# An earlier activation table and earlier masks, a smaller source of zeros, and eight identity products ahead of the loop, in a gated recurrence with a top-k expert layer

## The chip, the cores and the metric

The kernel runs on one core of a Trainium2 chip. A core has five engines with a queue of their own each: TensorE (PE in the profile, with its weight loads as PEld), VectorE (DVE), ScalarE (ACT), GpSimd (POOL) and SyncE (SP). Here SyncE computes nothing; its queue issues almost all DMA transfers. The metric is the device time of one execution in microseconds (us), as the median of several runs; lower is better.

## The reference: what is computed

The first stage is a gated linear recurrence over 4 sequences of 5056 steps and 256 channels; the second treats its 4 x 5056 = 20224 results as tokens of a layer with 8 experts, where each expert keeps only the 80 tokens with the highest gate.

```python
def _attn_ref(x, f_logit, lower_bound):
    sig = 1.0 / (1.0 + np.exp(-f_logit))
    f = lower_bound[None, None, :] + (1.0 - lower_bound[None, None, :]) * sig
    i = 1.0 - f
    for t in range(S):
        h = f[:, t] * h + i[:, t] * x[:, t]
        y[:, t] = h

def _moe_ref(x, w_gate, w1, w2, capacity):          # x: (20224, 256), capacity 80
    logits = x @ w_gate                              # 8 experts
    expert_idx = np.argmax(logits, axis=1)
    gate_w = softmax(logits)[np.arange(N), expert_idx]
    out = np.zeros((N, D))
    for e in range(E):
        tok_idx = np.where(expert_idx == e)[0]
        tok_idx = tok_idx[np.argpartition(-gate_w[tok_idx], capacity)[:capacity]]
        h = np.maximum(x[tok_idx] @ w1[e], 0.0)      # w1[e]: 256 x 1024
        out[tok_idx] = gate_w[tok_idx, None] * (h @ w2[e])   # w2[e]: 1024 x 256
```

All values are 32-bit floats. At most 640 of the 20224 rows of the output are not zero, so the kernel writes zeros over the whole output, 20.7 MB, and then scatters the experts' rows over them.

## The kernel before

**Recurrence.** The work is cut into 40 units: 10 groups of up to 512 steps, times 4 sequences. A unit is a pair of loads, `f_t` and `x_t`, 512 KB each (448 KB in the last group), `load` at lines 214 to 221. Then `gate` (ScalarE: sigmoid, line 225), `enter` (GpSimd: product with x, line 229), `to_channels` (TensorE: 8 transposes of each through the identity into PSUM tiles `sp` and `up`, line 236), `decay` (ScalarE, line 247), `scan` (VectorE: the recurrence itself, line 253, into `h_all`, which stays on the chip) and `logits` (TensorE, line 265). The loop at lines 404 to 422 writes the order out by hand: in turn n it loads unit n + 3, gates n + 2, transposes n + 1, scans n. The pool of loads has four buffers for each of the two tiles, so a fifth load waits until the transposes have read the first.

**Before the loop.** `setup` at lines 186 to 212 prepares constants: VectorE scales the gate weights by `omlb`, which waits for two small loads (`lb`, `wg`, issued on ScalarE's queue at lines 79 and 83), then builds the masks `place`, `mine`, `before`, `mates`. GpSimd fills an on-chip tile `zero`, and ScalarE's queue writes it to `z_dram` at line 194, a scratch tensor of 128 x 2048 floats (1 MB) in the chip's memory, which is from then on the source of all zeros. ScalarE's queue holds, in order: the loads of `lb` and `wg`, the write of `z_dram`, the load of the sigmoid's table, the first sigmoid.

**Zeros.** The output seen as 128 rows of 158 x 256 floats is cleared in 20 column blocks of 8 x 256 floats, 1 MB each (the last 768 KB). `clear(k, q)` copies one quarter of a block, 32 of its rows and 256 KB; `clear(k)` copies a whole block, from the 128 rows of `z_dram` to the 128 rows of the block. Both copy from memory to memory on SyncE's queue, in rows of 8 KB. From turn 8 of the loop on, one quarter is written in each turn, and 12 at its last load: 40 quarters. `clear_rest` at line 468 writes the ten blocks that are left, whole: nine of 1 MB and one of 768 KB.

**Experts.** The selection (lines 500 to 581) follows the last unit. The weights come in transfers of 512 KB, two for each `w1[e]` and two for each `w2[e]`, through a ring of seven buffers (`wring`, line 444). SyncE's queue holds them so: six transfers (`w1[0]`, `w2[0]`, `w1[1]`, lines 466 and 467), then the ten whole blocks of zeros (`clear_rest`), and then the other 26 transfers, beginning with the two of `w1[2]`, then `w2[1]`, `w1[3]`, `w2[2]` and so on. Each waits for its buffer of the ring. For each expert, `gather` copies 80 columns out of `h_all` (line 625), `hidden` multiplies by `w1` (line 643), `relu` follows on ScalarE, `result` multiplies by `w2` (line 658), `finish` scales, and `scatter` writes 80 rows into the output by an indirect DMA of GpSimd (line 667); the first one must come after all the zeros. TensorE's order is hidden(0), result(0), hidden(1), hidden(2), result(1), hidden(3), result(2), to result(7).

`busy` at line 167 issues products of the identity with itself whose result nobody reads; before the change it is called in the selection only.

Of the kernel before, what the change touches and what calls it, by code (L numbers as in the profile page):

```python
# [9 lines left out]
F32 = mybir.dt.float32  # L10
# [4 lines left out]
ALU = mybir.AluOpType  # L15
ACT = mybir.ActivationFunctionType
PSUM = bass.MemoryType.PSUM
P = 128
# [5 lines left out]
def kernel(  # L24
# [11 lines left out]
    nc = tc.nc  # L36
    B, S, D = x.shape
    E, _, F = w1.shape
    N = B * S
    DC = D // P  # L40
    FC = F // P
    R = 4
# [27 lines left out]
    consts = ctx.enter_context(tc.tile_pool(name="consts", bufs=1))  # L70
    dram = ctx.enter_context(tc.tile_pool(name="dram", bufs=1, space=bass.MemoryType.DRAM))
# [3 lines left out]
    ident = consts.tile([P, P], F32, name="ident")  # L75
    make_identity(nc, ident)

    lb = consts.tile([P, DC], F32, name="lb")
    nc.scalar.dma_start(out=lb, in_=lower_bound.rearrange("(o p) -> p o", p=P))
    LC = P // R  # L80
    wg = consts.tile([P, DC, LC], F32, name="wg")
    nc.vector.memset(wg, 0.0)
    nc.scalar.dma_start(out=wg[:, :, :E], in_=w_gate.rearrange("(o p) e -> p o e", p=P))
    omlb = consts.tile([P, DC], F32, name="omlb")
    nomlb = consts.tile([P, DC], F32, name="nomlb")
# [13 lines left out]
    before = consts.tile([P, P], F32, name="before")  # L99
    mine = consts.tile([P, E], F32, name="mine")  # L100
    place = consts.tile([P, C], F32, name="place")
    ones = consts.tile([P, 1], F32, name="ones")
    nc.vector.memset(ones, 1.0)

    ahead = consts.tile([P, K + DEEP - 1], F32, name="ahead")
    nc.gpsimd.iota(ahead, pattern=[[1, K + DEEP - 1]], base=1 - DEEP, channel_multiplier=0,
# [23 lines left out]
    doubt = consts.tile([1, 1], I32, name="doubt")  # L130


    consts.tile([P, 8], F32, name="pad")


    hpool = tc.alloc_tile_pool(name="hpool", bufs=1, side="right")
    h_all = hpool.tile([P, DC, N], F32, name="h_all")
    ctx.enter_context(tc.manual_schedule())
# [1 line left out]

    ZR = 8
    ZC = 512
    z_dram = dram.tile([P, ZR * D], F32, name="z_dram")
    out_z = out.rearrange("(p k) d -> p (k d)", p=P)
    clears = range(0, N // P, ZR)
    QP = P // R
    zeros = [(k, q) for k in clears for q in range(R)]


    def clear(k, q=None):  # L150
        n = min(ZR, N // P - k) * D
        rows = slice(0, P) if q is None else ds(q * QP, QP)
        nc.sync.dma_start(out=out_z[rows, ds(k * D, n)], in_=z_dram[rows, :n])

    def clear_some(m):
        for k, q in zeros[:m]:
            clear(k, q)
        del zeros[:m]

    def clear_rest():  # L160
        clear_some(len(zeros) % R)
        for k, _ in zeros[::R]:
            clear(k)
        zeros.clear()


    def busy(pool, m, tag):
        warm = pool.tile([P, P], F32, name="warm", tag=tag)
        for _ in range(m):
            nc.tensor.matmul(warm, ident, ident, start=True, stop=True)  # L170

    with tc.tile_pool(name="ld", bufs=4) as ld, \
# [11 lines left out]
            return b * S + first(g)  # L184

        def setup():
            nc.vector.tensor_scalar(omlb, lb, -1.0, 1.0, ALU.mult, ALU.add)
            nc.vector.tensor_scalar(nomlb, lb, 1.0, -1.0, ALU.mult, ALU.add)
            for o in range(DC):
                nc.vector.tensor_scalar_mul(wg[:, o], wg[:, o], omlb[:, ds(o, 1)])  # L190
            zero = gsm.tile([P, ZC], F32, name="zero", tag="ls")
            nc.gpsimd.memset(zero, 0.0)
            m = ZR * D // ZC
            nc.scalar.dma_start(out=z_dram.rearrange("p (m z) -> p m z", m=m),
                                in_=zero.unsqueeze(1).broadcast_to([P, m, ZC]))

            col_i = gsm.tile([P, P], I32, name="col_i", tag="shift")
            nc.gpsimd.iota(col_i, pattern=[[1, P]], base=0, channel_multiplier=0)
            col_f = gsm.tile([P, P], F32, name="col_f", tag="gm", bufs=2)
            nc.vector.tensor_single_scalar(row_i[:, 1:2], row_i[:, 0:1], shift_c,  # L200
                                           op=ALU.arith_shift_right)
            nc.vector.tensor_single_scalar(row_i[:, 2:3], row_i[:, 0:1], C - 1,
                                           op=ALU.bitwise_and)
            nc.vector.tensor_copy(row_f, row_i)
            nc.vector.tensor_copy(col_f, col_i)
            nc.vector.tensor_scalar(place, col_f[:, :C], row_f[:, 2:3], None, ALU.is_equal)
            nc.vector.tensor_scalar(mine, col_f[:, :E], row_f[:, 1:2], None, ALU.is_equal)
            nc.vector.tensor_scalar(before, col_f, row_f[:, 0:1], None, ALU.is_gt)
            nc.vector.tensor_single_scalar(col_i, col_i, shift_c, op=ALU.arith_shift_right)
            nc.vector.tensor_copy(col_f, col_i)  # L210
            nc.vector.tensor_scalar(mates, col_f, row_f[:, 1:2], None, ALU.is_equal)
            nc.vector.tensor_tensor(before, before, mates, ALU.mult)

        def load(n):
            g, b = divmod(n, B)
            fs[n] = ld.tile([P, R, D], F32, name="f_t", tag="f_t")
            nc.sync.dma_start(
                out=fs[n][:run(g)], in_=tiles(f_logit, b, g))
            xs[n] = ld.tile([P, R, D], F32, name="x_t", tag="x_t")
            nc.sync.dma_start(  # L220
                out=xs[n][:run(g)], in_=tiles(x, b, g))
# [9 lines left out]
        def to_channels(n, src, dst, pool, tag):  # L231
            k = run(n // B)
            for o in range(DC):
                ps = pool.tile([P, G], F32, name=tag, tag=tag)
                for r in range(R):
                    nc.tensor.transpose(ps[:, ds(r * k, k)], src[n][:, r, ds(o * P, P)],  # L236
                                        ident[:k, :k])
                dst[n, o] = ps[:, :R * k]
            del src[n]
# [29 lines left out]
        def aside(g):  # L269
            k = run(g)  # L270
            lss[g] = gsm.tile([P, B * P], F32, name="ls", tag="ls")[:, :B * k]
            nc.scalar.copy(lss[g].rearrange("p (b t) -> p b t", b=B), lgs.pop(g)[:, :, :k])  # L272
# [19 lines left out]
        def shifted(g):  # L292
            by_token(g)
            n_p = run(g)
            lg, _ = lts[g]
            full = [n_p, C, E]
            if g == begin(g):
                shs[g] = gsm.tile([P, per_batch, C, E], F32, name="shift", tag="shift")
                ohs[g] = gsm.tile([P, per_batch, C, E], BF16, name="oh", tag="oh", bufs=2)
                if any(run(k) < P for k in range(*batch_of(g))):  # L300
                    nc.gpsimd.memset(shs[g], 0.0)
            mx = gsm.tile([P, C], F32, name="mx", tag="mx")[:n_p]
            nc.vector.tensor_reduce(mx, lg, AX.X, ALU.max)
            nc.vector.tensor_tensor(lg, lg, mx.unsqueeze(2).broadcast_to(full), ALU.subtract)
            nc.scalar.copy(shs[begin(g)][:n_p, g - begin(g)], lg)
# [78 lines left out]
        def unit(f, m):  # L384
            if 0 <= m < n_unit:
                f(m)
# [5 lines left out]
        def chosen(g):  # L392
            choice(g)
            if g in batches:
                of_batch.extend(work(*batches[g]))

        def some_of(jobs, k):
            while jobs and k:
                for f in jobs.pop(0):
                    f()  # L400
                k -= 1

        setup()
        for n in range(-AHEAD, n_unit):
            unit(load, n + AHEAD)
            unit(gate, n + 2)
            unit(enter, n + 2)
            unit(lambda m: to_channels(m, sts, sps, pss, "sp"), n + 1)
            unit(lambda m: to_channels(m, uts, ups, psu, "up"), n + 1)
            unit(decay, n + 1)  # L410
            unit(scan, n)
            some_of(of_group, 1)
            some_of(of_batch, 1 if n < n_unit - 2 else 2)
            unit(logits, n - 1)
            if n + AHEAD == n_unit - 1:
                clear_some(3 * R)
            elif 2 * B <= n < n_unit - AHEAD:
                clear_some(1)
            if n > 0 and n % B == 0:
                g = n // B - 1  # L420
                of_group += [[lambda g=g: aside(g)], [lambda g=g: shifted(g)],
                             [lambda g=g: chosen(g)]]
# [301 lines left out]
    with tc.If(unsure > 0):  # L724
        with tc.tile_pool(name="all", bufs=1) as sel, \
# [23 lines left out]
            sp = psa.tile([K, 2, E], F32, name="slots")  # L749
# [10 lines left out]
            for e in range(E):  # L760
                nc.gpsimd.indirect_dma_start(
                    out=tok[:, ds(e, 1)], out_offset=None, in_=id_list,
# [7 lines left out]
            for k in clears:  # L770
                clear(k)
# [33 lines left out]
```

## Time and profile before

| | us |
|---|---|
| median of three runs | 241.88 |
| lowest and highest run | 241.83 and 242.76 |
| the profiled execution, its own time | 241.2 |
| the profiled execution, its span from first to last instruction | 239.1 |
| TensorE busy in the span | 204.7 |
| VectorE busy in the span | 162.0 |
| ScalarE busy in the span | 140.2 |
| GpSimd busy in the span | 135.3 |

The span is what the views below divide; the execution's own time is 2.1 us longer than it. The mean granted clock of TensorE was 0.986. SyncE's DMA queue (q1) moved 78.92 MB, and its packets took 94.8% of the span on 16 engines. A few transfers by kind, from the page's part on DMA issues (the column at the end is the median time from issue to landing):

```profile
w_sb<-in_moe_w_dram SPq DMA_DIRECT2D x32, 512.0 KB, 5.9
out_dram<-z_dram SPq DMA_DIRECT2D x40, 256.0 KB, 6.7
z_dram<-zero ACTq DMA_DIRECT2D x1, 1024.0 KB
```

A row of that part names target and source, the queue that issues, how many there are and the size of each.

### The profile page before, as it was taken

To read this page: it belongs to the slowest core of one execution; us is meant where nothing else is said; L and a number is where in the kernel's file an instruction comes from. 1 tells how busy PE (TensorE), PEld (TensorE's weight loads), DVE (VectorE), ACT (ScalarE), POOL (GpSimd) and SP (SyncE) were. 2 spreads that over 40 slices of the span, in tenths; PEclk is the share of its full clock that TensorE was granted. 3 is DMA by queue.
4 is the path that set the end of the run, shared out by engine and by line. 5 is a ranking of instruction groups with operands and counts; after the bars stand their busy time and mean duration, and the time that the engine had idled before them with its cause. 6 is when DMAs were issued, how large, how long until landed. Compare 5 with 4: busy or idle time off the path is not lost.

```text
span 239.1 us, 6235 instructions
## 1 busy us (share of the span) xinstructions
PE 204.7 (86%) x1883; PEld 162.4 (68%) x1883; DVE 162.0 (68%) x434; ACT 140.2 (59%) x437; POOL 135.3 (57%) x273
## 2 busy tenths in 40 slices
PE   0579999999999689999978994986969999999990
PEld 0567667776767457766755771985867988888850
DVE  0897859697897769699876968676466625556010
ACT  0667768687777959676795843050465477445100
POOL 3658778768677487967657841011457266661111
PEclk9999999999999999999999999799999999999997
DMA  7999999999999999999999999999999999999500
GB/s 173 372 388 385 382 385 387 390 390 394 389 389 390 393 391 384 387 395 394 387 346 321 372 314 326 419 355 325 311 331 287 380 386 374 313 333 327 163 18 22
DMA packets 59386, 81.11 MB, mean 339 GB/s; under 512 B 3280, under 2 KB 52048, under 8 KB 56912
## 3 DMA queue, kind: packets, MB, share of 16 engines
q1 hardware_dynamic: 57888, 78.92, 94.8%
q10 hardware_dynamic: 1072, 1.06, 1.3%
q0 software_dynamic: 384, 0.66, 0.8%
q8 instruction: 17, 0.28, 0.4%
q14 instruction: 25, 0.20, 0.3%
HBM read 78.91 MB, written 22.41 MB: 424 GB/s over the span
## 4 chain that ended last, share of the span: by engine, by line
PE 38%; DMA 22%; issue 14%; ACT 9%; DVE 7%; POOL 5%; SPq 1%; POOLq 1%; DVEq 0%; ACTq 0%
PE lg L265 11%; DMA out_dram<-y,goal 10%; PE sp L236 10%; PE up L236 7%; PE warm L170 5%; DMA x_t<-in_x_dram 5%; DMA w_sb<-in_moe_w_dram 4%; ACT h_all L247 4%; DVE h_all L253 3%; DMA f_t<-in_f_logit_dram 3%; POOL x_t L229 3%; PE lt L280 2%; ACT ls L272 1%; ACT signs L533 1%; ACT f_t L225 1%
## 5 line engine op out<-in xcount | busy, mean ns | idle before, releaser
L229 POOL TENSOR_TENSOR x_t<-f_t,x_t 128x1024 f32<-128x1024 f32 (+1 forms) x40 | 94.9, 2381 | 39.6 <-ACT f_t L225 21.9
L253 DVE TENSOR_TENSOR_SCAN h_all<-h_all,up 128x512 f32<-128x512 f32 (+1 forms) x80 | 95.1, 1240 | 6.0 <-ACT h_all L247 4.6
L247 ACT ACTIVATE h_all<-sp,nomlb 128x512 f32<-128x512 f32 (+1 forms) x80 | 50.0, 678 | 16.3 <-PE sp L236 16.3
L236 PE MATMUL sp<-ident,f_t 128*128 128x128 f32 (+1 forms) x320 | 45.3, 285 | 10.3 <-ACT f_t L225 8.0
L236 PEld LDWEIGHTS sp<-ident,f_t 128*128 128x128 f32 (+1 forms) x320 | 35.5, 145 | 27.0 <-issue 20.5
L265 PE MATMUL lg<-h_all,wg 128*32 128x128 f32 (+1 forms) x640 | 43.5, 401 | 5.2 <-ACT ls L272 3.7
L236 PE MATMUL up<-ident,x_t 128*128 128x128 f32 (+1 forms) x320 | 43.1, 276 | 4.8 <-POOL x_t L229 3.3
L225 ACT ACTIVATE f_t<-f_t 128x1024 f32<-128x1024 f32 (+1 forms) x40 | 42.6, 1064 | 6.7 <-DMA f_t<-in_f_logit_dram 6.2
L236 PEld LDWEIGHTS up<-ident,x_t 128*128 128x128 f32 (+1 forms) x320 | 36.2, 143 | 7.1 <-POOL x_t L229 4.6
L625 ACT COPY xe<-h_all 128x2 f32 x256 | 25.4, 190 | 14.8 <-issue 8.9
L625 POOL COPY xe<-h_all 128x2 f32 x192 | 24.6, 200 | 14.3 <-issue 12.6
L625 DVE COPY xe<-h_all 128x2 f32 x192 | 22.7, 179 | 12.7 <-issue 12.7
L643 PEld LDWEIGHTS h_ps<-xt,w_sb 128*128 128x128 f32 x256 | 29.6, 192 | 1.9 <-issue 1.3
L643 PE MATMUL h_ps<-xt,w_sb 128*128 128x80 f32 x256 | 29.8, 275 | 1.2 <-issue 1.2
L265 PEld LDWEIGHTS lg<-h_all,wg 128*32 128x32 f32 x640 | 18.1, 118 | 18.1 <-ACT ls L272 5.9
L658 PE MATMUL y_ps<-w_sb,hid 128*80 128x256 f32 x128 | 28.8, 380 | 1.4 <-ACT hid L651 1.4
L658 PEld LDWEIGHTS y_ps<-w_sb,hid 128*80 128x80 f32 x128 | 18.7, 150 | 9.0 <-ACT hid L651 1.5
L667 POOL DMA_INDIRECT out_dram<-y,goal x8 | 7.5, 941 | 25.2 <-DVE y L664 16.0
L170 PE MATMUL warm<-ident 128*128 128x128 f32 x136 | 17.8, 294 | 0.0
L170 PEld LDWEIGHTS warm<-ident 128*128 128x128 f32 x136 | 17.3, 209 | 0.1
L664 DVE TENSOR_SCALAR y<-y_ps,gsl 80x256 f32<-80x256 f32 x8 | 3.8, 478 | 16.6 <-PE y_ps L658 16.6
L651 ACT ACTIVATE hid<-h_ps 128x320 f32<-128x320 f32 x16 | 6.6, 429 | 11.5 <-PE h_ps L643 10.4
(110 smaller groups left out, 100.3 us busy)
## 6 DMA issues: line engine op xcount, KB each, us to landing
f_t<-in_f_logit_dram SPq DMA_DIRECT2D x36, 512.0 KB, 7.0
x_t<-in_x_dram SPq DMA_DIRECT2D x36, 512.0 KB, 7.5
w_sb<-in_moe_w_dram SPq DMA_DIRECT2D x32, 512.0 KB, 5.9
out_dram<-z_dram SPq DMA_DIRECT2D x40, 256.0 KB, 6.7
out_dram<-z_dram SPq DMA_DIRECT2D x9, 1024.0 KB, 19.2
f_t<-in_f_logit_dram SPq DMA_DIRECT2D x4, 448.0 KB, 6.9
x_t<-in_x_dram SPq DMA_DIRECT2D x4, 448.0 KB, 6.6
z_dram<-zero ACTq DMA_DIRECT2D x1, 1024.0 KB
```

The source lines that it names most:

```text
L170: nc.tensor.matmul(warm, ident, ident, start=True, stop=True)
L225: nc.scalar.activation(s_t, s_t, ACT.Sigmoid, scale=-1.0)
L229: nc.gpsimd.tensor_tensor(u_t, sts[n], u_t, ALU.mult)
L236: nc.tensor.transpose(ps[:, ds(r * k, k)], src[n][:, r, ds(o * P, P)], ident[:k, :k])
L247: nc.scalar.activation(columns(n, o), sps.pop((n, o)), ACT.Identity, scale=nomlb[:, ds(o, 1)], bias=1.0)
L253: nc.vector.tensor_tensor_scan(h, h, ups.pop((n, o)), h_all[:, o, ds(spot(n) - 1, 1)] if n >= B else 0.0, ALU.mult, ALU.add)
L265: nc.tensor.matmul(lgs[g][ds(r * LC, LC), b, :k], wg[:, o], columns(n, o)[:, r::R], start=o == 0, stop=o == DC - 1, skip_group_check=True)
L625: copy(X[e][:, :, ds(k + j, 1)], h_all[:, :, ds(v, 1)])
L643: nc.tensor.matmul(h_ps[:, c], halves[i][:, o, ds(c * P, P)], xt[:, o], start=o == 0, stop=o == DC - 1, skip_group_check=True)
L651: nc.scalar.activation(HID[e][:, ds(i * CH, CH)], ps[i], ACT.Relu)
L658: nc.tensor.matmul(y_ps, hid[:, c], halves[c // CH][:, c % CH], start=c == 0, stop=c == FC - 1)
L667: nc.gpsimd.indirect_dma_start(out=out, out_offset=bass.IndirectOffsetOnAxis(ap=goal[:, ds(e, 1)], axis=0), in_=Y.pop(e), in_offset=None, ...
```

## The change

There are four edits. Line numbers from here to the end of the diff are those of the kernel before unless said otherwise.

1. A one-column tile of ones is filled first, and ScalarE applies the sigmoid to it into a tile `early` that nobody reads; so ScalarE's queue now holds the load of `lb`, the load of the sigmoid's table, this small sigmoid, the load of `wg`, and then the first unit's sigmoid.
2. In `setup`, VectorE builds the masks first and scales the gate weights afterwards.
3. `z_dram` shrinks from 128 to 32 rows (1 MB to 256 KB). It is written on SyncE's queue by the new function `source`, in turn 0 of the loop after the load of unit 3, instead of on ScalarE's queue in `setup`. Every quarter `clear(k, q)` now reads the same 32 rows. A whole block `clear(k)` reads these 32 rows four times over: its source has four copies with a step of zero as its first dimension, then 32 rows; its target is the block's 128 rows in the built program.
4. At the end of `setup`, `busy(pss, 8, "sp")` issues eight identity products on TensorE ahead of the first transposes.

A tile named `pad`, which nothing used, is dropped.

```diff
     ident = consts.tile([P, P], F32, name="ident")
     make_identity(nc, ident)
 
+
+    ones = consts.tile([P, 1], F32, name="ones")
+    nc.vector.memset(ones, 1.0)
+    early = consts.tile([P, 1], F32, name="early")
+    nc.scalar.activation(early, ones, ACT.Sigmoid)
+
     lb = consts.tile([P, DC], F32, name="lb")
...
-    ones = consts.tile([P, 1], F32, name="ones")
-    nc.vector.memset(ones, 1.0)
...
-    consts.tile([P, 8], F32, name="pad")
...
     ZR = 8
     ZC = 512
-    z_dram = dram.tile([P, ZR * D], F32, name="z_dram")
+    QP = P // R
+    z_dram = dram.tile([QP, ZR * D], F32, name="z_dram")
...
     def clear(k, q=None):
         n = min(ZR, N // P - k) * D
-        rows = slice(0, P) if q is None else ds(q * QP, QP)
-        nc.sync.dma_start(out=out_z[rows, ds(k * D, n)], in_=z_dram[rows, :n])
+        if q is None:
+            nc.sync.dma_start(
+                out=out_z[:, ds(k * D, n)].rearrange("(q p) d -> q p d", p=QP),
+                in_=z_dram[:, :n].unsqueeze(0).broadcast_to([R, QP, n]))
+        else:
+            nc.sync.dma_start(out=out_z[ds(q * QP, QP), ds(k * D, n)], in_=z_dram[:, :n])
...
         def setup():
-            nc.vector.tensor_scalar(omlb, lb, -1.0, 1.0, ALU.mult, ALU.add)
-            nc.vector.tensor_scalar(nomlb, lb, 1.0, -1.0, ALU.mult, ALU.add)
-            for o in range(DC):
-                nc.vector.tensor_scalar_mul(wg[:, o], wg[:, o], omlb[:, ds(o, 1)])
-            zero = gsm.tile([P, ZC], F32, name="zero", tag="ls")
             nc.gpsimd.memset(zero, 0.0)
-            m = ZR * D // ZC
-            nc.scalar.dma_start(out=z_dram.rearrange("p (m z) -> p m z", m=m),
-                                in_=zero.unsqueeze(1).broadcast_to([P, m, ZC]))
...
             nc.vector.tensor_tensor(before, before, mates, ALU.mult)
+            nc.vector.tensor_scalar(omlb, lb, -1.0, 1.0, ALU.mult, ALU.add)
+            nc.vector.tensor_scalar(nomlb, lb, 1.0, -1.0, ALU.mult, ALU.add)
+            for o in range(DC):
+                nc.vector.tensor_scalar_mul(wg[:, o], wg[:, o], omlb[:, ds(o, 1)])
+            busy(pss, 8, "sp")
+
+        zero = gsm.tile([P, ZC], F32, name="zero", tag="ls")
+
+        def source():
+            m = ZR * D // ZC
+            nc.sync.dma_start(out=z_dram.rearrange("p (m z) -> p m z", m=m),
+                              in_=zero[:QP].unsqueeze(1).broadcast_to([QP, m, ZC]))
...
         for n in range(-AHEAD, n_unit):
             unit(load, n + AHEAD)
+            if n == 0:
+                source()
             unit(gate, n + 2)
```

More of the change, by code (lines that the diff above doesn't have):

```diff
@@ L142 @@
     ZC = 512
-    z_dram = dram.tile([P, ZR * D], F32, name="z_dram")
+    QP = P // R
+    z_dram = dram.tile([QP, ZR * D], F32, name="z_dram")
     out_z = out.rearrange("(p k) d -> p (k d)", p=P)
     clears = range(0, N // P, ZR)
-    QP = P // R
     zeros = [(k, q) for k in clears for q in range(R)]
```

## The prediction

> **What bounds the kernel now.** I read the 40 slices of the page first, to see which resource is full where. Each digit of the DMA row is the busy share of a slice of 6 us in tenths; below it stand the GB/s that all DMA moved.
>
> ```profile
> DMA  7999999999999999999999999999999999999500
> GB/s 173 372 388 385 382 385 387 390 390 394 389 389 390 393 391 384 387 395 394 387 346 321 372 314 326 419 355 325 311 331 287 380 386 374 313 333 327 163 18 22
> ```
>
> The DMA engines are full from 6 to 222 us, at some 390 GB/s in the recurrence. So an early transfer removed makes all later ones earlier, and the zeros are on the path wherever something stands behind them in SyncE's queue. Next the order of SyncE's issues around the end of the recurrence (start, duration, engine, line, what, how many):
>
> ```profile
> 142.10 0.91 SPq L456 DMA_DIRECT2D w_sb<-in_moe_w_dram  x2
> 143.06 1.02 SPq L460 DMA_DIRECT2D w_sb<-in_moe_w_dram  x2
> 144.12 1.58 SPq L456 DMA_DIRECT2D w_sb<-in_moe_w_dram  x2
> 145.74 15.06 SPq L153 DMA_DIRECT2D out_dram<-z_dram  x10
> 163.75 12.85 SPq L456 DMA_DIRECT2D w_sb<-in_moe_w_dram  x2
> ```
>
> Six weight transfers, the ten whole blocks of zeros, and behind them, issued at 163.75 and 176.24, the two halves of w1[2]. Then the chain of waits from 172 us on, where the wait that ended last is named:
>
> ```profile
> 174.22 2.00 PE h_ps L643 x16
> 176.22 0.02 issue
> 176.24 10.40 DMA w_sb<-in_moe_w_dram
> ```
>
> and TensorE's timeline there:
>
> ```profile
> 183.12 3.80 PE L643 MATMUL h_ps<-xt,w_sb 128*128 128x80 f32 x32
> 186.85 0.19 PE L699 MATMUL total<-doubts,ones 128*1 128x4 f32 x2
> 186.97 3.80 PE L643 MATMUL h_ps<-xt,w_sb 128*128 128x80 f32 x32
> ```
>
> The second half of w1[2] lands at 176.24 + 10.40 = 186.64, and hidden(2) starts at 186.97. From there TensorE works without a gap: one expert is 3.5 us of line 643 and 3.5 of line 658, and the span ends 239.1 - 186.97 = 52.1 us after hidden(2) starts. So the zeros' drain sets when the experts go on already now, and only just: hidden(1) ended at 186.9 as well. There is no slack left for the ten blocks. Last, how fast they drain, from the windows in 6 us stretches (busy time of each engine, then clock, DMA share, GB/s):
>
> ```profile
> 150.00:156.00 6.00, 6.00 (x41) 6.00 (x41) 3.63 (x16) 0.58 (x2) 0.25 (x1) 0.72 1.05 421
> 168.00:174.00 6.00, 5.06 (x44) 4.86 (x44) 3.24 (x26) 3.34 (x33) 3.07 (x24) 1.00 0.99 306
> ```
>
> 421 GB/s over 16 engines is 26.3 GB/s for one, the best of any stretch with zeros in it; 306 is 19.1 for one, with nothing but zeros running on all 16.
>
> **What the Trainium skill says.** The page "DMA: Bandwidth & Descriptors", section "Why a DMA increments its semaphore by 16 and not by 1", says that a copy issued from SyncE is cut over k of the 16 engines, where k is the largest number up to 16 that divides the slowest dimension, other than one of size 1, of both sides. Its "Rules for kernel authors" add that a leading broadcast of c copies with step zero confines the whole transfer to at most c engines. No transfer of the kernel before has such a dimension (all have 32, 112, 128 or 512 rows outermost), so this trace neither supports nor contradicts it. The same page, "Queues, rings and completion order", says that each queue has a ring on each engine, consumed in order; the trace agrees as far as w1[2] landed only after the zeros ahead of it. The page "TensorE: Matmul & The Clock Gate", Part 1, says that TensorE falls to half its clock when idle for a few us and needs some 3.4 us of work to come back. The trace shows that at its start: the first 16 transposes, from 8.03 us, took 1.94 and 1.97 us for eight, later ones 1.09.
>
> **The change part by part.**
>
> *Whole blocks from a source with four copies in front.* This part decides. The source's slowest dimension becomes 4 while the target keeps 128, so by the rule k = 4: engines 0 to 3 carry all ten blocks. Their bytes: 9 x 1,048,576 + 786,432 = 10.22 MB. One engine gets 2.556 MB. At 26.3 GB/s that is 97.2 us, at 19.1 it is 133.8. I take 97.2: the low rate came with 16 engines reading and writing memory together, while four of them put a quarter of that load on it; the packet records of the trace also show 309 ns for a row of 8 KB where quarters run beside loads, which is 26.5 GB/s. It can't be less unless an engine is faster than in any stretch here. Every later weight transfer needs all 16 engines, so it waits in the rings of engines 0 to 3 for the last block.
>
> When do they start? The packets of the sixth weight transfer end and those of the first block begin between 151.8 and 153.3 us; I take 152.5, and 2.0 less for the edit below: 150.5. The last block ends at 150.5 + 97.2 = 247.7. The twelve other engines hold up to seven weight transfers done in three quarters by then (the ring's buffers are free, since hidden(0), result(0) and hidden(1) need only the first six). Engines 0 to 3 owe 32 KB each for the first half of w1[2], 1.25 us, and I add 0.5 for its landing (the last zeros' packet ended at 184.6, that transfer landed at 160.3 + 24.6 = 184.9): hidden(2) can start at 249.5. The next halves follow each 1.25 us, TensorE needs one in 1.75 (3.5 for a pair), so it doesn't wait again. The rest is the 52.1 us above. TensorE has then been idle for 60 us and is cold; at half speed over its first 3.4 us or somewhat more it loses 2 to 4 us, I take 2.5. Span: 249.5 + 52.1 + 2.5 = 304.1.
>
> *768 KB less into the source, and later.* 786,432 bytes at 390 GB/s are 2.0 us of a full DMA stream, saved near 5 us and, since the stream stays full, kept until the blocks begin. Bounds: nothing, if the recurrence is held by TensorE (SyncE waited 33.4 us in all for transposes to free a buffer), and 2.7 us if the whole megabyte leaves the first loads' way. The 256 KB move past eight loads on SyncE's queue; their issue costs 0.5 us there, just when the next load waits for a buffer until 10.42 us anyway. The issue leaves ScalarE's queue (0.59 us at 4.92). Every quarter reads the same 32 rows: same bytes, still 32 rows outermost, so k = 16, nothing.
>
> *Early table.* The table's 1.28 us at 5.54 move to about 1 us, beside the first loads' flight, so the first sigmoid (6.83) can start up to 1.3 us earlier, with the moved issue up to 1.9. The load of wg is issued behind it, about 2 us later; its first reader is the scaling, then logits at 18.70, so it has 8 us of cover. What is late next is the stream of loads; so I count nothing, with at most 1.9 us as the gain.
>
> *Masks first.* Two of VectorE's mask operations took 2.38 and 2.28 us while GpSimd's products ran; built from 2.4 us on they take some 0.3 each and are over by about 5 us. The first scan (13.36) then waits for its transposes, done at about 12.4: 1 us at the start, again inside a full stream. The scaling moves behind; ScalarE needs nomlb at 9.46, VectorE has it by 5.5. Nothing.
>
> *Eight identity products.* Cold they take about 0.25 us each, 2 us from 1.4 us on: over by 4, while the first transpose may come at 6 to 8, so that TensorE can have gone cold again. Between a gain of 1 us and a loss of nothing, since TensorE was idle to 8.03; I count nothing. Dropping pad costs nothing.
>
> Sum: span 304.1, and with the 2.1 us around it 306.2 for the execution, against its own 241.2. The median shown is 0.7 above that execution; I round to 306.
>
> **Rivals.**
>
> *The blocks are spread over all 16 engines all the same* (faster). If the split follows the target's 128 rows, or the two sides are matched before the split, the ten blocks drain as before in some 32 us, and only the 2.0 us of the smaller source show: 241.88 - 2.0 = 239.9, 239 with a part of the front's gains. For it: the built target has 128 rows, and the front edits all point the right way. Against it: the rule is stated for both sides, with this very case as its example. It decides from the point where the drain isn't longer than before, since w1[2] lands at its use already.
>
> *Four engines, at less than their best rate.* All four read the same 32 rows at the same time and could meet at the same place in memory. With 19.1 GB/s for one the drain is 133.8, 36.6 more: 343.
>
> *Another number of engines.* With 8 the drain is 48.6 us, w1[2] lands near 201, and the sum gives 258; with 2 it is 194.4 us, and 404.
>
> *Hidden anyway.* The zeros could drain slowly beside the experts' work. But the first scatter must come after them, and only experts 0 and 1 have weights ahead of the blocks: the cover ends at 186.9.
>
> **How the numbers follow.** Forecast 306: 0.76. Sixteen engines, 239 to 240: 0.11. Four engines at the low rate, up to 343: 0.10. Other numbers: 0.03. The likeliest case has its own range of 299 to 316 (start of the blocks 2 us either way, cold start and landing 3, drain up to 5% longer). To leave out no more than 2 in 10 I reach into the low-rate case: 297 to 328. A measurement of this kernel tells about 0.5% from no change; of the 0.11, 0.08 are faster by more and 0.03 within it. All else is slower: 0.89.
>
> **What would show it.** Right: ten blocks with landing times that grow to 80 us or so, DMA share near a quarter from 155 to 247 at about 105 GB/s, TensorE empty from 187 to about 249, hidden(2) longer at first, then seven us for an expert. The recurrence's last scan some 2 us earlier than at 146.2 shows the smaller source. Wrong: DMA share still at 9 tenths after 155 means sixteen engines; a drain longer than 105 us means the reads meet; weights landing during the drain mean that the rings don't hold them back.

## The result, and the profile after

The changed kernel takes 308.60 us (median, 307.28 to 308.69); the kernel before took 242.06 in the same set of runs. The ratio is 1.273, with a 95% interval of 1.269 to 1.277: 66.5 us slower. The profiled execution took 308.69 us with a span of 306.8. Line numbers have moved: the changed kernel has hidden at L654, result at L669 and the whole blocks at L154, where the kernel before has L643, L658 and L153.

Its 40 slices, each 7.67 us long now: the granted clock of TensorE in tenths, the DMA engines' busy share in tenths, and the GB/s.

```profile
PEclk9599999999999999999799998555555555999998
DMA  7999999999999999999822222222234495799910
GB/s 218 387 383 385 387 390 395 384 392 393 392 388 388 394 390 335 281 358 323 315 108 109 106 107 105 106 109 107 107 142 175 157 305 196 240 315 331 312 32 28
```

In slices 21 to 29 the DMA engines are busy a quarter of the time at 105 to 109 GB/s. Over the same stretch the kernel before had 9 tenths and more than 280 GB/s. One window of the same stretch as before, with the DMA share and the GB/s in the last two columns:

```profile
168.00:174.00 6.00, 4.85 (x44) 4.69 (x43) 3.83 (x31) 3.72 (x39) 4.49 (x36) 1.00 0.25 105
```

A share of 0.25 is four engines of sixteen, and 105 GB/s over four is 26 for each, as much as the prediction had found for one engine at its best. Next SyncE's queue (start, duration, line, target and source, how many):

```profile
142.51 1.82 SPq L467 DMA_DIRECT2D w_sb<-in_moe_w_dram  x2
144.37 63.20 SPq L154 DMA_DIRECT2D out_dram<-z_dram  x10
207.61 25.29 SPq L467 DMA_DIRECT2D w_sb<-in_moe_w_dram  x2
233.00 11.94 SPq L471 DMA_DIRECT2D w_sb<-in_moe_w_dram  x2
```

Issuing the ten blocks took 15.06 us before and takes 63.20 now, and the two halves of w1[2] behind them are issued from 207.61 on instead of from 163.75. In the packet records, which hold each row that an engine moved, the blocks' rows run from 150.8 to 247.8, 97.0 us; before, from 151.8 to 184.6. TensorE's timeline shows who waits for this:

```profile
184.63 0.19 PE L710 MATMUL total<-doubts,ones 128*1 128x4 f32 x2
249.53 7.09 PE L654 MATMUL h_ps<-xt,w_sb 128*128 128x80 f32 x32 [64.71 <-DMA w_sb<-in_moe_w_dram]
256.41 5.58 PE L669 MATMUL y_ps<-w_sb,hid 128*80 128x256 f32 x16
261.83 3.69 PE L654 MATMUL h_ps<-xt,w_sb 128*128 128x80 f32 x32
```

In front of hidden(2) TensorE stands idle for 64.71 us and waits for w1[2]. Then hidden(2) takes 7.09 us and result(1) 5.58; from there on the pairs run at 3.69 and 3.62, as in the kernel before. The rest of the kernel, up to 144 us, came out 2.3 us earlier: the last scan ended at 143.97 instead of 146.26.

### The profile page after: what moved, and what is told of

It reads as the page before. It is cut to its first block, busy times and chain, and to the rows that moved or that the text cites. A ratio compares the mean times of both kernels' runs of the same rounds, so it can differ in the third digit from the quotient of the medians.

```text
span 306.8 us, 6267 instructions
## 1 busy us (share of the span) xinstructions
PE 212.9 (69%) x1899; PEld 170.4 (56%) x1899; DVE 160.7 (52%) x434; ACT 141.0 (46%) x438; POOL 135.3 (44%) x273
## 4 chain that ended last, share of the span: by engine, by line
PE 39%; DMA 23%; SPq 20%; ACT 9%; issue 3%; DVE 3%; POOL 2%; POOLq 0%; ACTq 0%; DVEq 0%
SPq L154 20%; DMA w_sb<-in_moe_w_dram 16%; PE y_ps L669 9%; PE h_ps L654 8%; PE lg L274 8%; PE sp L245 7%; PE up L245 6%; DMA f_t<-in_f_logit_dram 5%; ACT h_all L256 4%; ACT f_t L234 2%; DMA x_t<-in_x_dram 2%; DVE h_all L262 2%; POOL x_t L238 1%; ACT ls L281 1%; PE lt L289 1%
## 5 line engine op out<-in xcount | busy, mean ns | idle before, releaser
L654 PE MATMUL h_ps<-xt,w_sb 128*128 128x80 f32 x256 | 33.1, 293 | 65.9 <-DMA w_sb<-in_moe_w_dram 64.7
L654 PEld LDWEIGHTS h_ps<-xt,w_sb 128*128 128x128 f32 x256 | 32.9, 209 | 66.6 <-issue 66.1
L678 POOL DMA_INDIRECT out_dram<-y,goal x8 | 7.5, 938 | 95.1 <-DMA w_sb<-in_moe_w_dram 64.7
L245 PE MATMUL sp<-ident,f_t 128*128 128x128 f32 (+1 forms) x320 | 44.5, 282 | 3.7 <-ACT h_all L256 2.3
L245 PEld LDWEIGHTS sp<-ident,f_t 128*128 128x128 f32 (+1 forms) x320 | 35.0, 143 | 20.4 <-issue 12.5
L245 PEld LDWEIGHTS up<-ident,x_t 128*128 128x128 f32 (+1 forms) x320 | 37.1, 145 | 6.3 <-POOL x_t L238 4.3
L669 PE MATMUL y_ps<-w_sb,hid 128*80 128x256 f32 x128 | 30.8, 398 | 1.4 <-ACT hid L662 1.4
L669 PEld LDWEIGHTS y_ps<-w_sb,hid 128*80 128x80 f32 x128 | 19.7, 159 | 10.0 <-ACT hid L662 1.5
L175 PE MATMUL warm<-ident 128*128 128x128 f32 x152 | 21.2, 305 | 1.4 <-POOL ident masks.py:199 1.4
L175 PEld LDWEIGHTS warm<-ident 128*128 128x128 f32 x152 | 20.5, 220 | 1.5 <-POOL ident masks.py:199 1.4
```

What stands on the lines that cost most here:

```text
L654: nc.tensor.matmul(h_ps[:, c], halves[i][:, o, ds(c * P, P)], xt[:, o], start=o == 0, stop=o == DC - 1, skip_group_check=True)
L669: nc.tensor.matmul(y_ps, hid[:, c], halves[c // CH][:, c % CH], start=c == 0, stop=c == FC - 1)
L678: nc.gpsimd.indirect_dma_start(out=out, out_offset=bass.IndirectOffsetOnAxis(ap=goal[:, ds(e, 1)], axis=0), in_=Y.pop(e), in_offset=None, ...
```

## The experiments

They ask four things: whether the order of the dimensions makes the loss and all of it; whether the number of engines follows the leading dimension; what made the tail after hidden(2) longer than before; and what the other edits are worth once the loss is gone. Beside them the kernel before was measured again, with medians of 241.87 to 242.30; every ratio below is to it.

**Rows first.** The whole-block copy with its two dimensions exchanged on both sides:

```diff
-                out=out_z[:, ds(k * D, n)].rearrange("(q p) d -> q p d", p=QP),
-                in_=z_dram[:, :n].unsqueeze(0).broadcast_to([R, QP, n]))
+                out=out_z[:, ds(k * D, n)].rearrange("(q p) d -> p q d", p=QP),
+                in_=z_dram[:, :n].unsqueeze(1).broadcast_to([QP, R, n]))
```

> The changed kernel, but the whole-block copies name the 32 rows first and the four copies second, on both sides; bytes, source rows and queue order are unchanged. Theory (the leading dimension of 4 confined the copies to four engines): all 16 engines drain the blocks in about 32 us as in the kernel before, TensorE's gap of 64.7 us goes, and the time is 239 to 240.5 us, a little under the kernel before. Rival one (four reads of the same 32 rows meet in memory, wherever they run): the drain stays well over 60 us and the time over 270. Rival two (the front edits or the late source hold the stages after them): near 308.

Measured: 240.05 us, ratio 0.990 (0.9876 to 0.9924). The drain lasts from 150.5 to 184.0 in the packet records, and TensorE's gap is gone:

```profile
186.15 0.19 PE L710 MATMUL total<-doubts,ones 128*1 128x4 f32 x2
186.28 3.80 PE L654 MATMUL h_ps<-xt,w_sb 128*128 128x80 f32 x32
```

So the same bytes from the same 32 rows, in the same place of the queue, cost 68.5 us less with 32 as the leading dimension. Both rivals fall. This version also beats the kernel before, by 1.0%.

**Eight copies.** The broadcast stays in front, but with eight copies of 16 rows:

```diff
-                out=out_z[:, ds(k * D, n)].rearrange("(q p) d -> q p d", p=QP),
-                in_=z_dram[:, :n].unsqueeze(0).broadcast_to([R, QP, n]))
+                out=out_z[:, ds(k * D, n)].rearrange("(q p) d -> q p d", p=QP // 2),
+                in_=z_dram[:QP // 2, :n].unsqueeze(0).broadcast_to([2 * R, QP // 2, n]))
```

> The changed kernel with a whole block read as eight copies of 16 rows, the copies first: the leading dimension is 8 instead of 4, the bytes are the same. Theory (as many engines as the leading dimension): 10.22 MB over 8 engines at 26.3 GB/s drain in 48.6 us, from about 150.6 to 199.2; hidden(2) starts near 201, TensorE is cold again, so 201 + 57.3 + 2 = 260 us. Rival (any leading broadcast falls back to four engines, or the reads of few rows meet): 308 or more.

Measured: 262.89 us, ratio 1.087 (1.0825 to 1.0914), and in the window of before

```profile
168.00:174.00 6.00, 5.27 (x46) 5.11 (x46) 3.31 (x26) 3.12 (x32) 3.05 (x24) 0.98 0.49 203
```

A share of 0.49 is eight engines. The drain took 51.8 us (150.5 to 202.3) and not 48.6, so hidden(2) started at 204.16 and not near 201; the tail behind it was 56.0 us, a little shorter than the 57.3 that had been taken over. The number of engines follows the leading dimension: 4, 8, and 16 for 32.

**The form alone, in the kernel before.** The source stays 128 rows and 1 MB, written as before; only the whole blocks read its first 32 rows four times:

```diff
+        if q is None:
+            nc.sync.dma_start(
+                out=out_z[:, ds(k * D, n)].rearrange("(q p) d -> q p d", p=QP),
+                in_=z_dram[:QP, :n].unsqueeze(0).broadcast_to([R, QP, n]))
+            return
```

> The kernel before with one edit: its whole-block copies read the first 32 rows of the 1 MB source four times over, the four copies first. Theory (this form alone makes the loss): blocks start at 152.5, drain in 97.2, end at 249.7; hidden(2) 1.8 later, then 57.3 us as in the changed kernel, and 2: about 311 us. Rival (the loss needs the small source, its late write or the front edits): 242 us.

Measured: 310.66 us, ratio 1.282 (1.2786 to 1.2853). TensorE has the same gap in front of hidden(2):

```profile
252.16 7.09 PE L648 MATMUL h_ps<-xt,w_sb 128*128 128x80 f32 x32 [64.24 <-DMA w_sb<-in_moe_w_dram]
```

None of the other edits is needed for the loss.

**TensorE kept at work over the drain.** In the changed kernel, identity products between hidden(1) and hidden(2), first 275 of them:

```diff
                 nc.tensor.matmul(total, ones, doubts[:, :4], start=True, stop=True)
+                busy(psl, 275, "kept")
```

> The changed kernel with 275 identity products on TensorE between hidden(1) and hidden(2), where it has nothing to do; at 0.227 us each they last 62 us. Theory (the 5.2 us by which the tail after hidden(2) is longer than before, 57.3 against 52.1, are TensorE at half clock): hidden(2) takes 3.8 us instead of 7.1, result(1) 3.6 instead of 5.6, and the time is 303 to 304. Rival (weights arrive late behind the blocks and stretch the tail): no change, 308.

Measured: 305.39 us, but the runs spread from 302.59 to 307.92. In the profiled one the products ended 2.12 us before hidden(2), the record of the granted clock stood at half from 250.86 to 257.69, and hidden(2) took 5.67. So this was not decided; the gap had to be closed, with 286 products:

> The changed kernel with 286 identity products between hidden(1) and hidden(2), 64.2 us of them, so that no gap of 2 us is left ahead of hidden(2). Theory (half clock is all of the tail's 5.2 us): 303 to 304 in every run, hidden(2) and result(1) at 3.8 and 3.6 us. Rival (late weights are a part of it): above 305 with TensorE at full clock.

Measured: 303.73 us (303.55 to 303.96), 4.9 less than the changed kernel. TensorE's timeline:

```profile
184.40 64.14 PE L175 MATMUL warm<-ident 128*128 128x128 f32 x572
249.46 3.80 PE L654 MATMUL h_ps<-xt,w_sb 128*128 128x80 f32 x32 [0.92 <-DMA w_sb<-in_moe_w_dram]
253.09 3.62 PE L669 MATMUL y_ps<-w_sb,hid 128*80 128x256 f32 x16
```

Hidden(2) starts where it did (249.46 and 249.53), and the span of 301.6 ends 52.1 us later, exactly as in the kernel before. The whole lengthening of the tail was the clock; no weights came late.

**The later weights on another queue.** In the changed kernel, the 26 transfers behind the blocks are issued from ScalarE's queue:

```diff
-                    w[key] = weights(*key)
+                    w[key] = weights(*key, nc.scalar)
```

> The changed kernel with the 26 weight transfers behind the blocks issued from ScalarE's queue instead of SyncE's. Theory (the rings of engines 0 to 3 belong to SyncE's queue and hold later transfers back in order): w1[2] lands long before the blocks end, hidden(2) starts before 200 us, and the first scatter, which needs all zeros, becomes the wait at about 255 to 265; the time is 300 to 316. Rival (the engines themselves are held by the zeros, whatever the queue): hidden(2) near 249 as before.

Measured, in a single execution: 343.39 us. Hidden(2) did start at 187.25, as the theory has it, but for another reason: only one block of zeros had been under way until then, and its rows ended at 160.1. SyncE's second block was issued only at 196.91. In the built program the transfers of both queues take eight completion semaphores (counters that tell when a transfer has landed) in turn, and the one of this block was still held by a moved transfer, the first half of w2[2], issued at 193.19. SyncE's queue waited for moved transfers 71.2 us in all:

```profile
SPq L154 <- DMA w_sb<-in_moe_w_dram: 71.2, 7, 51.2
```

What follows in the same trace does decide between theory and rival. The other nine blocks drained from 200.4 to 292.1, and in the packet records all 14 weight transfers that ScalarE's queue had issued by 202.29 were done at 239.1, in the middle of the zeros: from 212 to 224 us, 138 of their rows ran beside 137 rows of zeros. So the four engines with work from two queues serve both, and the rival falls: in the changed kernel the weights stand behind the zeros because they stand behind them in SyncE's own queue. The move as it stands costs 35 us all the same, since the zeros start late and the first scatter waits for them until 293.39.

**What the other edits are worth.** These start from the rows-first kernel (240.05 us) and take one edit back each. First the source, 1 MB on ScalarE's queue in setup again, each copy reading its own rows of it:

```diff
-    z_dram = dram.tile([QP, ZR * D], F32, name="z_dram")
+    z_dram = dram.tile([P, ZR * D], F32, name="z_dram")
...
             nc.gpsimd.memset(zero, 0.0)
+            m = ZR * D // ZC
+            nc.scalar.dma_start(out=z_dram.rearrange("p (m z) -> p m z", m=m),
+                                in_=zero.unsqueeze(1).broadcast_to([P, m, ZC]))
...
-            if n == 0:
-                source()
```

> The kernel with rows first (16 engines for every copy), but with the 1 MB source of 128 rows, written on ScalarE's queue in setup as in the kernel before; the early table, the masks first and the eight products stay. Theory (the smaller, later source is what the rest of the change gains, 2.0 us of a full DMA stream): about 242, the kernel before. Rival (the front edits gain it): about 240, as rows first.

Measured: 242.21 us, ratio 1.0016 (0.9995 to 1.0038). The front edits gain nothing without the smaller source.

Then the eight products, left out:

```diff
-            busy(pss, 8, "sp")
```

> The kernel with rows first, without the eight identity products in front. Theory (TensorE has slack at the start and goes cold again in between): no change, 240 within 0.6. Rival (warm first transposes carry the start): 241 or more; other rival (the products move the half-clock stretch into the recurrence and cost there): below 239.5.

Measured: 240.19 us. They do nothing for the time.

Then the scaling of the gate weights ahead of the masks again:

```diff
             nc.gpsimd.memset(zero, 0.0)
+            nc.vector.tensor_scalar(omlb, lb, -1.0, 1.0, ALU.mult, ALU.add)
...
             nc.vector.tensor_tensor(before, before, mates, ALU.mult)
-            nc.vector.tensor_scalar(omlb, lb, -1.0, 1.0, ALU.mult, ALU.add)
```

> The kernel with rows first, with VectorE's scaling ahead of the masks again, so that two mask operations run beside GpSimd's products. Theory (hidden by the full DMA stream): no change, 240 within 0.6. Rival (the first scan carries the start): about 241 to 242, since the first scan moves back by 2 us or so.

Measured: 245.32 us, ratio 1.0138 (1.0092 to 1.0184): the theory falls, and by more than its rival had asked. VectorE's timeline at the start of this run:

```profile
7.61 2.34 DVE L205 CAST row_f<-row_i 128x3 f32<-128x3 int32 x1
10.39 2.40 DVE L209 TENSOR_SCALAR before<-col_f,row_f 128x128 f32<-128x128 f32 x1
13.22 2.26 DVE L212 TENSOR_SCALAR mates<-col_f,row_f 128x128 f32<-128x128 f32 x1
15.72 4.55 DVE L262 TENSOR_TENSOR_SCAN h_all<-h_all,up 128x512 f32<-128x512 f32 x4
```

GpSimd's timeline beside it, with the products:

```profile
7.58 2.34 POOL L238 TENSOR_TENSOR x_t<-f_t,x_t 128x1024 f32<-128x1024 f32 x1 [5.15 <-DMA x_t<-in_x_dram]
10.30 2.40 POOL L238 TENSOR_TENSOR x_t<-f_t,x_t 128x1024 f32<-128x1024 f32 x1 [0.38 <-DMA x_t<-in_x_dram]
13.02 2.38 POOL L238 TENSOR_TENSOR x_t<-f_t,x_t 128x1024 f32<-128x1024 f32 x1 [0.31 <-DMA x_t<-in_x_dram]
```

Three mask operations take 2.26 to 2.40 us, each beside one of GpSimd's products, where the same three take 0.28 to 0.53 in front. The Trainium skill says of this, on the page "SBUF — State Buffer" under "Who interferes with whom", that VectorE and GpSimd share a pair of ports, that casts and `tensor_scalar` are among the VectorE operations that can need it, and that whichever comes second then waits for the whole of the other's instruction; the lengths agree.

The first scan starts at 15.72 instead of 10.78. The next transposes wait for it, and the load behind them waits for their buffer: SyncE waits up to 4.0 us, and the load of x_t at 14.10 moves to 18.14.

```profile
16.99 1.11 PE L245 MATMUL up<-ident,x_t 128*128 128x128 f32 x4 [2.49 <-DVE h_all L262]
```

So the DMA stream has a hole. Of the two rows below, of the page's GB/s, the first is the rows-first kernel and the second this run, from its fourth to its eighth figure below 355. An estimate from these five figures: 278 GB/s less in sum over slices of 6 us are 1.7 MB, or 4.3 us at 390 GB/s, most of the 5.3 us lost.

```profile
GB/s 159 382 387 382 386 382 390 390 388 392 391 389 394 388 378 394 386 390 391 395 287 305 372 313 353 421 345 336 310 313 307 393 385 335 304 335 310 190 19 22
```

```profile
GB/s 162 384 387 262 353 347 336 354 390 388 390 394 389 395 384 389 393 389 389 394 326 325 367 341 326 422 345 333 314 326 294 387 362 311 316 315 318 187 18 22
```

One thing is not separated: in this run TensorE stood at half clock from 8.48 to 22.14, where the record of the rows-first kernel has the full clock from 13.02 on. A part of the loss can be that.

Then the small source alone in the kernel before, read with the rows first, with table, masks and products as they were:

```diff
-            zero = gsm.tile([P, ZC], F32, name="zero", tag="ls")
             nc.gpsimd.memset(zero, 0.0)
-            m = ZR * D // ZC
-            nc.scalar.dma_start(out=z_dram.rearrange("p (m z) -> p m z", m=m),
-                                in_=zero.unsqueeze(1).broadcast_to([P, m, ZC]))
...
+            if n == 0:
+                source()
```

> The kernel before with the small, later source alone, read with the rows first; table, masks and products as in the kernel before. Theory from the run with the masks last (once the source's issue leaves ScalarE's queue, the first sigmoid starts at about 5.3, GpSimd's products start earlier and hold three of the masks for 2.3 us each, so that the first scan comes at 15.7 and the stream of loads runs dry): about 245, slower than the kernel before. Rival (as the prediction had it, the smaller source gains 2.0 us by itself): 240.

Measured: 244.33 us, ratio 1.0121 (1.0073 to 1.0169). The smaller source by itself makes the kernel slower. In its trace the sigmoid's table loads early with no edit to the table, because the issue of the source, at 4.92 in the kernel before, no longer stands ahead of it on ScalarE's queue:

```profile
1.79 1.28 ACT L232 ACT_TABLE_LOAD   x1 [1.79 <-DVE ones L103]
5.38 1.06 ACT L232 ACTIVATE f_t<-f_t 128x1024 f32<-128x1024 f32 x1 [2.31 <-DMA f_t<-in_f_logit_dram]
```

GpSimd's products come earlier, three masks are caught, and the first scan starts at 15.22, where the kernel before had two caught and 13.36. Here half clock stands on record only from 15.92 to 19.33, so a long stretch of it is not needed for a loss.

Last the early table, left out:

```diff
-    early = consts.tile([P, 1], F32, name="early")
-    nc.scalar.activation(early, ones, ACT.Sigmoid)
```

> The kernel with rows first, without the early sigmoid, so that ScalarE loads its table when the first unit's sigmoid comes. Theory (the front is hidden by a full DMA stream): no change, 240 within 0.6. Rival (the first sigmoid carries the start): 241.3, since 1.3 us of table load come back.

Measured: 250.19 us, ratio 1.0342 (1.0313 to 1.0371), which neither side had. Its front is that of the rows-first kernel (first sigmoid at 5.28 against 5.34, first scan at 10.72 against 10.78), but from the second slice to the twentieth, through the whole recurrence, its loads run below it:

```profile
GB/s 174 350 358 347 349 347 369 358 371 368 364 366 372 366 365 368 370 367 365 370 293 280 264 387 309 384 383 338 333 318 276 366 365 360 329 332 298 234 18 21
```

In the built programs the tile `early` takes 32 bytes of each row of the on-chip memory. Without it the eight load buffers, and the tiles that share their place later, begin 32 bytes lower, the first at 25568 instead of 25600. The kernel before has an unused tile of that size, which the change dropped; it was put back:

```diff
+    consts.tile([P, 8], F32, name="pad")
```

> The kernel with rows first and without the early sigmoid once more, but with the unused 32-byte tile of the kernel before put back, so that the load buffers begin at 25600 bytes again and not at 25568. Theory (the 10 us that the run without the early sigmoid lost came from the buffers' place, since its front ran as before and its loads at 350 to 370 GB/s instead of 385 to 395): 240 within 0.6, and 385 to 395 GB/s again. Rival (the early table itself is worth 10 us): 250.

Measured: 240.34 us, and

```profile
GB/s 155 382 388 382 385 382 387 389 390 389 394 390 392 389 379 393 391 388 390 394 311 319 371 308 380 417 345 330 317 319 307 388 354 322 305 315 318 175 18 22
```

So the early table is worth nothing in time here, and its tile is worth 10 us as a spacer.

## Why the prediction was right

Forecast were 306 us, and 308.60 were measured. The mechanism was right at each step that decides; three terms beside it were not.

**Four engines.** Right, with its numbers: the drain was put at 97.2 us and took 97.0; its end at 247.7 and came at 247.8; hidden(2) at 249.5 and started at 249.53. A little luck is in the drain's start. It was put at 152.5 - 2.0 = 150.5 and came at 150.8, but the blocks of the kernel before had begun at 151.8 already, so the edit brought it forward by 1.0 us and not by 2.0. The runs with 8 and with 32 in front, and the form alone in the kernel before, show that the leading dimension does it. The bound of 133.8 us for reads that meet in memory did not come up: in the packet records a row of 8 KB took 310 ns on average with four engines and 313 with eight, against 389 in the drain on 16 before.

**The rest behind hidden(2).** The 52.1 us taken over from the kernel before hold exactly (the run with TensorE at work). The term that was mis-sized is the cold start: 2.5 us predicted, with 4 as the most, and 57.3 - 52.1 = 5.2 measured. The trace's clock record stands at half from 188.70 to 260.38, so TensorE worked 10.85 us at half clock, not 3.4 us or somewhat more. The Trainium skill's page "TensorE: Matmul & The Clock Gate", Part 1, gives some 3.4 us; here the measurement decides. This is the 2.7 us by which the span of 306.8 exceeds the 304.1 of the sum. The trace of the kernel before could have warned of it, for a group of eight transposes that began 4 us after the first ones was still slow:

```profile
12.21 1.78 PE L236 MATMUL sp<-ident,f_t 128*128 128x128 f32 x8
```

**Weights waiting in the rings.** Right in kind, too large in number. The prediction had seven transfers done in three quarters by the end of the drain. The packets say four at most: by 246 us, 384 of the 512 rows of w1[2], and fewer than three quarters of those of w2[1]. SyncE itself stood still at its issues, 9.1 to 9.9 us for each of six blocks, so the first row of w1[2] ran only at 228.66. What had been issued then did wait behind the zeros: three quarters of w1[2] ran by 235.6, and the last quarter from 246.7 to 248.9. It cost nothing more, since TensorE was the bound again after w1[2].

**The smaller source, 2.0 us.** Right for the sum, wrong as it was put together. Rows first gains 242.30 - 240.05 = 2.2 us on the runs of before beside it, and taking the source back loses all of it. But the prediction counted the masks as nothing, looking at the first scan of the kernel before. Moving the source off ScalarE's queue brings the first sigmoid 1.5 us forward by itself, and this brings GpSimd's products among the masks. So the smaller source alone makes the kernel 2.3 us slower than before (244.33 against 242.05) and not 2.0 us faster, and in the rows-first form the kernel with the scaling ahead of the masks is 5.3 us slower than with the masks first (245.32 against 240.05). The term that was wrong is the masks', "again inside a full stream", counted at nothing: the stream does not stay full when the first scan comes 5 us late, since four buffers are all that the loads have.

**Early table and products.** Counted at nothing, and nothing they are (240.34 and 240.19 against 240.05). Three details differ. The issue of the source was seen ahead of the table, but not that without it the table comes early on its own. The load of wg was to be issued 2 us later behind the table; it was issued at 1.33, beside the load of the table, against 1.27 before. And the products took 3.46 us, not 2. "Dropping pad costs nothing" held by luck: `early` fills the 32 bytes that `pad` had kept, and with neither the kernel takes 250.19 us.

**The rivals.** Sixteen engines all the same is what the rows-first form gives, 240.05 where 239 to 240 stood; in the form of the change it didn't happen.

## What to carry to other kernels

Before a copy is made from a repeated source, look at the first dimension of both sides as the program has them, not only at the target's: a broadcast of four in front cost 68 us here, and exchanging two dimensions gave it back. When an edit frees a queue, follow what starts earlier on it and which engine that will meet, for the gain can turn into a loss elsewhere. And an experiment that removes a tile moves every tile behind it: keep its place before reading the time.

## What the runs showed of the hardware

- Copies of zeros over four, eight and sixteen engines moved a row of 8 KB in 310, 313 and 389 ns on average. When a second queue had work for the same four engines, they moved one of its rows of 1 or 2 KB for each row of zeros (138 beside 137 in 12 us).
- Load buffers that begin at 25568 instead of 25600 bytes: the loads run at 347 to 372 GB/s instead of 379 to 394, and the kernel takes 250.19 us instead of 240.34. Only tiles behind the 32 bytes moved; why the place matters was not tested.
- After 64.7 us of rest TensorE stayed at half clock for 10.85 us of unbroken work; after rests of 17.66 us (eight copies), 64.24 (the form alone) and 96.86 (the other queue) it was 8.48, 11.33 and 9.60. In one trace a rest of 2.12 us was followed by 6.83 us at half clock, and in another a rest of 0.92 us was not.
- Issues on SyncE's queue hold SyncE itself while four engines are behind: 9.1 to 9.9 us for a block and 20.4 for the first half of w1[2], against 0.5 to 0.7 for a block before.
